# Down side of the second MoE: sum group in up-side banks, VectorE in GpSimd's place, and earlier splits

## The chip, the cores and the metric

One NeuronCore of a Trainium2 chip runs the whole program. The metric is the device time of one execution in microseconds; three executions of the kernel before were timed, and one more was profiled.

## The reference, cut to what matters

```python
x = attention(q, k, v, M_prev, z_prev, beta)      # 2304 tokens x 512
h = x @ w_in                                      # first MoE, 2048 wide
x = (h * sigmoid(h)) @ w_out
g = x @ w_gate                                    # second MoE, 1536 wide
val = x @ w_val
return ((g * sigmoid(g)) * val) @ w_out2          # 2304 x 512, float32
```

The change is in the last three lines, and in the pace at which the weights for them are prepared while the first MoE still runs.

## The kernel before, in words

The attention and the first MoE fill the first 680 us. While they run, the weights of the second MoE are read, combined and split into high and low halves, and written back to DRAM (`prep_w2`). A generator, `open_w2`, hands out that preparation over the last part of the first MoE: one step at every second call, set by `late=2` in the table `CFG`.

The second MoE works on three blocks of 768 tokens. Both of its sides are done with seven products of half-size matrices in place of eight (Strassen's scheme as Winograd has it), and each product is three matmuls: high by high, high by low and low by high half.

The up side has 12 slices `j` of 128 gate and 128 value columns. For each, `up(i, j, p)` issues the seven products, 6 matmuls of 384 columns each. Their sums live in PSUM: a tile of two banks (tag `o`, two tiles), and single banks `b` and `d` (two each, `sum_bank`). ScalarE copies a sum into a bank on which further products are added (L1205), VectorE adds others (L1213, L1219). A bank on which products are added to copied data needs a first matmul that marks it as written: the seed (L1182), for the first two slices of the first block. The gated results `r` are 128 x 384 tiles, two per slice (L1197).

The down side takes two slices together: for `q` from 0 to 5 the four tiles of slices 2q and 2q+1 are the quarters a11, a12, a21, a22. `halved` makes the three combinations of them on GpSimd (L1250 to L1252). `split_p` splits a tile into `ph` (a ScalarE cast, L1241) and `pl`, the low half (L1242, on GpSimd for the first product and for odd q, on VectorE for the others); S4 also takes a subtraction on VectorE (L1237). The products come in the order A11, S1, A12, S2, S4, S3, A22, six pieces each, 42 pieces a block. A piece is 9 matmuls of 256 columns (`piece_mm`, L1263): three token tiles by three halves. The products form four groups of sums, each in one tile `o` of two banks: A11 then A12, S1 then S4, S2 then S3, and A22. As there are two such tiles, the third group takes the one that the first leaves, and the first group ends with a ScalarE copy of the output (L1316).

The pieces of the first product are split in the up side; those of the others six pieces ahead, in rings of six `ph` and six `pl`. The last product of the last block is finished token tile by token tile, each followed by an addition (L1300) and a store.

TensorE's order is written out by `pe_order`: the products of neighbouring slices are interleaved, the first three pieces of a down side lie between the last products of the up side, and the last two between the first products of the next block. The order on the other engines and on SyncE's queue is made by a scheduler at build time. Weights come from DRAM by `stream` through a ring of eight 512 KB buffers, in the order of use (L1145); those of S2 and S4 are loaded once (`load_res`, L1155) and stay. `y_prep` loads and splits the inputs of the next block (L1022 to L1047) on ScalarE and VectorE.

Of the kernel before, what the change touches and what calls it, by code (L numbers as in the profile page):

```python
# [57 lines left out]
    late=2,  # L58
    res='S2 S4',
# [35 lines left out]
def kernel(  # L95
# [993 lines left out]
    def open_2():  # L1089
        ph2["xp"].close()  # L1090
        ph1.close()
        for nm in ("pr", "pp", "tp", "op", "res"):
# [3 lines left out]
    RES = CFG["res"].split()  # L1096
# [22 lines left out]
    def needs():  # L1119
        for n, (kind, i, x, y) in enumerate(pos):  # L1120
            if kind == "u":
                key = ("u", i, x, (0, 1, 1, 0, 2, 2, 3)[y])
            elif DQ[x] not in RES:
                key = ("d", i, x, y // 2)
            else:
                continue
# [21 lines left out]

    res = {}

    def load_res(g):
        for nm in RES:
            if g == 0:
                res[nm] = ph2["res"].tile([P, 2 * NJ2, 256], F32, name="res" + nm)
            nc.sync.dma_start(out=res[nm][:, 4 * g:4 * g + 4], in_=wdo[BW[nm], g])  # L1155
# [3 lines left out]
    def up(i, j, p):  # L1159
# [17 lines left out]
        def seeded(tag):  # L1177

            t = sum_bank(tag, "g" + tag)
            if i == 0 and j < 2:  # L1180
# [43 lines left out]
        else:  # L1224
# [3 lines left out]
            if j % 2:  # L1228
                halved(i, j // 2)

    pt, s1, queue, split = {}, {}, [], [0]

    def split_p(i, n, q):
        nm = DQ[n]
        a11, a12, a21, a22 = pt[0, 2 * q], pt[0, 2 * q + 1], pt[1, 2 * q], pt[1, 2 * q + 1]
        if nm == "S4":
            nc.vector.tensor_sub(a12, a12, a21)  # L1237
        src = dict(A11=a11, S1=s1.get(q), A12=a12, S2=a21, S4=a12, S3=a11, A22=a22)[nm]
        ph = ph2["pp"].tile([P, HT], F32R, tag="ph", name="ph", bufs=NJ2)
        pl = ph2["pp"].tile([P, HT], F32R, tag="pl", name="pl", bufs=NJ2)  # L1240
        nc.scalar.copy(ph, src)  # L1241
        (nc.gpsimd if n == 0 or q % 2 else nc.vector).tensor_sub(pl, src, f(ph))  # L1242
        return ph, pl

    def halved(i, q):

        queue.append(split_p(i, 0, q))
        a11, a21, a22 = pt[0, 2 * q], pt[1, 2 * q], pt[1, 2 * q + 1]
        s1[q] = ph2["pr"].tile([P, HT], F32, tag=f"s{q}", name="s1")
# [6 lines left out]
    def piece_mm(nm, g, q, pr, ts, begin, end):  # L1256
        ph, pl = pr
        w = res[nm][:, 2 * q:2 * q + 2] if nm in RES else streamed["d", g[0], DQ.index(nm), q // 2][:, 2 * (q % 2):2 * (q % 2) + 2]
        wh, wl = r_(w[:, 0]), r_(w[:, 1])
        for t in ts:  # L1260
            c = slice(P * t, P * t + P)
            for m, (a, x) in enumerate(((ph, wh), (ph, wl), (pl, wh))):
                nc.tensor.matmul(  # L1263
                    g[1][:, 256 * t:256 * t + 256], a[:, c], x, start=(begin and m == 0 and t != 1),
                    stop=(end and m == 2), skip_group_check=True,
                )

# [12 lines left out]
    def down(i, n, q):  # L1280
# [4 lines left out]
        if begin:  # L1285
            acc[G] = ph2["o"].tile([P, 1024], F32, tag="o", name=f"po{G}")[:, 0:3 * 256]
        g = acc[G]
        pr = queue.pop(0)
        if n == q == 0:
            split[0] = NJ2  # L1290
        if tail and q >= NJ2 // 2:
            late.append((q, pr))
# [3 lines left out]
            for t in range(HT // P):  # L1296
                for x, pr in late:
                    piece_mm(nm, (i, g), x, pr, (t,), False, x == q)
                c = slice(256 * t, 256 * t + 256)
                nc.vector.tensor_add(ot[:, c], g[:, c], snap["x"][:, c])  # L1300
                go(range(t, t + 1))
            return
        piece_mm(nm, (i, g), q, pr, range(HT // P), begin, q == NJ2 - 1)
        k = n * NJ2 + q
        while k > 2 and split[0] <= min(k + NJ2, len(DQ) * NJ2 - 1):
            queue.append(split_p(i, *divmod(split[0], NJ2)))
            split[0] += 1
# [4 lines left out]
        if nm in ("A11", "S1"):  # L1312
            nc.scalar.copy(s, g)
        elif nm == "A12":
            ot, go = put_out(i, 0, 0)
            nc.scalar.copy(ot, g)  # L1316
# [119 lines left out]
```

## Time and profile before

| | |
|---|---|
| median of 3 runs | 1096.02 us (1092.87 to 1096.34) |
| profiled execution | 1095.09 us, of which the span is 1092.9 |
| TensorE: matmul rows, weight loads | 1051.0 us (96%), 981.4 us (90%) |
| VectorE, ScalarE, GpSimd | 659.4, 554.8, 553.0 us |
| DMA | 252 MB, 231 GB/s on average |

The span is the time from the first to the last instruction. PE stands for TensorE's matmuls, PEld for its weight loads, which overlap them; DVE is VectorE, ACT ScalarE, POOL GpSimd, SP SyncE and SPq the queue of transfers that it issues. An engine's idle time before an instruction is put down to what it waited for last.

### The profile page before, as it was taken

The page shows a single profiled execution, that of the slowest core. Times are in us where ns is not written, and L with a number is a line of the kernel's source. Part 1 is how long each engine was busy: PE and PEld are TensorE (multiplying, and loading weights), DVE is VectorE, ACT ScalarE, POOL GpSimd, SP SyncE. Part 2 cuts the span into 40 slices and gives each one's busy share as a digit, 9 for nine tenths or more (in the row PEclk, how much of TensorE's full clock was granted, in tenths as well). Part 3 has the DMA queues.
Part 4 walks back from the last instruction along what each step waited for, and adds up shares of the span by engine and source line. Part 5 has one row for each costly group of instructions (what it writes and reads, how often), then busy time and mean ns, then how long its engine had stood idle before and what let it go on. Part 6 is the DMA issues. An engine that isn't in the chain of part 4 may idle for free.

```text
span 1092.9 us, 20747 instructions
## 1 busy us (share of the span) xinstructions
PE 1051.0 (96%) x7386; PEld 981.4 (90%) x7386; DVE 659.4 (60%) x1498; ACT 554.8 (51%) x1318; POOL 553.0 (51%) x622
## 2 busy tenths in 40 slices
PE   7889999999999998999999999999999999999998
PEld 5566888888999888998889999999999999999998
DVE  6897589996556656456757752344934449344443
ACT  6665677766655655546655542223532235322242
POOL 3676446577565565556644984122641226422253
PEclk8889999999999999999999999999999999999999
DMA  9967577565698554975537999877847778477771
GB/s 213 283 207 233 161 228 226 152 197 191 210 299 256 201 176 137 312 251 192 173 107 292 372 319 347 305 248 255 328 138 251 247 251 288 132 262 242 254 243 45
DMA packets 168103, 251.99 MB, mean 231 GB/s; under 512 B 76736, under 2 KB 114112, under 8 KB 168000
## 3 DMA queue, kind: packets, MB, share of 16 engines
q1 hardware_dynamic: 165824, 250.27, 69.3%
q8 instruction: 59, 0.97, 0.4%
q10 hardware_dynamic: 2176, 0.40, 0.2%
q14 instruction: 44, 0.36, 0.1%
HBM read 191.38 MB, written 59.24 MB: 229 GB/s over the span
## 4 chain that ended last, share of the span: by engine, by line
PE 68%; DVE 10%; DMA 7%; POOL 5%; issue 4%; ACT 2%; SPq 0%; POOLq 0%; ACTq 0%; DVEq 0%
PE h L825 12%; PE y L884 12%; PE po L1263 11%; PE oac L1171 10%; PE gb L1171 10%; PE gd L1171 3%; PE U L589 3%; PE pss L404 2%; PE pst L337 2%; DMA raw<-in_moe_w_val_dram 2%; POOL gl L835 1%; DMA raw<-in_moe_w_gate_dram 1%; DMA w<-wg 1%; POOL s L493 1%; DVE raw L702 1%
## 5 line engine op out<-in xcount | busy, mean ns | idle before, releaser
L825 PE MATMUL h<-xh,w 128*128 128x256 f32 (+1 forms) x1024 | 170.7, 305 | 7.3 <-ACT w L210 3.2
L884 PE MATMUL y<-gh,w 128*128 128x320 f32 (+1 forms) x1024 | 173.5, 305 | 3.6 <-DVE th L833 2.2
L1242 POOL TENSOR_TENSOR pl<-r,ph 128x384 fp32r<-128x384 f32 x63 | 69.1, 1100 | 199.4 <-ACT ph L1241 179.9
L835 POOL TENSOR_TENSOR gl<-th,gh 128x256 fp32r<-128x256 f32 (+1 forms) x128 | 111.4, 872 | 102.9 <-ACT gh L210 95.1
L825 PEld LDWEIGHTS h<-xh,w 128*128 128x128 f32 x1024 | 145.5, 191 | 15.2 <-ACT w L210 4.0
L884 PEld LDWEIGHTS y<-gh,w 128*128 128x128 f32 x1024 | 146.3, 190 | 10.1 <-DVE th L833 3.4
L1171 PE MATMUL gb<-yT,w 128*128 128x384 f32 x648 | 124.8, 336 | 0.0
L1171 PEld LDWEIGHTS gb<-yT,w 128*128 128x128 f32 x648 | 113.1, 188 | 0.0
L833 DVE SCALAR_TENSOR_TENSOR th<-th,h 128x256 f32<-128x256 f32 (+1 forms) x128 | 57.2, 449 | 74.8 <-ACT th L832 74.8
L1263 PE MATMUL po<-w,ph 128*128 128x256 f32 x540 | 98.2, 283 | 1.0 <-DVE ot L1300 1.0
L1241 ACT CAST ph<-r 128x384 fp32r<-128x384 f32 x108 | 55.0, 513 | 85.1 <-PE po L1263 45.7
L493 POOL TENSOR_TENSOR s<-s,r 128x128 f32<-128x128 f32 (+4 forms) x96 | 71.9, 775 | 49.7 <-DVE r L505 27.3
L884 PE MATMUL y<-gl,w 128*128 128x320 f32 (+1 forms) x512 | 94.0, 300 | 1.8 <-POOL gl L835 1.7
L825 PE MATMUL h<-xl,w 128*128 128x320 f32 (+1 forms) x512 | 92.8, 301 | 0.0
L460 ACT ACTIVATE s<-s,mn 128x128 f32<-128x128 f32 (+3 forms) x128 | 71.0, 556 | 31.9 <-DVE mn L456 31.4
L1263 PEld LDWEIGHTS po<-w,ph 128*128 128x128 f32 x540 | 84.9, 191 | 1.4 <-DVE ot L1300 1.4
L210 ACT CAST gh<-th 128x256 fp32r<-128x256 f32 (+1 forms) x128 | 55.1, 432 | 53.5 <-DVE th L833 41.6
L1171 PE MATMUL oac<-yB,w 128*128 128x384 f32 x432 | 81.3, 336 | 0.0
L884 PEld LDWEIGHTS y<-gl,w 128*128 128x128 f32 x512 | 76.6, 191 | 2.5 <-POOL gl L835 2.2
L1263 PE MATMUL po<-w,pl 128*128 128x256 f32 x270 | 76.4, 283 | 1.8 <-DVE pl L1242 1.8
L825 PEld LDWEIGHTS h<-xl,w 128*128 128x128 f32 x512 | 76.5, 191 | 1.7 <-issue 1.1
L1171 PEld LDWEIGHTS oac<-yB,w 128*128 128x128 f32 x432 | 75.4, 188 | 0.0
(165 smaller groups left out, 2228.5 us busy)
## 6 DMA issues: line engine op xcount, KB each, us to landing
w<-wg SPq DMA_DIRECT2D x108, 512.0 KB, 4.8
w<-wd SPq DMA_DIRECT2D x80, 512.0 KB, 5.4
wg<-wo SPq DMA_DIRECT2D x36, 512.0 KB, 3.4
wd<-w SPq DMA_DIRECT2D x32, 512.0 KB, 3.7
raw<-in_moe_w_out_dram SPq DMA_DIRECT2D x28, 512.0 KB, 4.9
w<-woT SPq DMA_DIRECT2D x27, 512.0 KB, 4.8
w<-wg SPq DMA_DIRECT2D x36, 256.0 KB, 4.9
w<-woB SPq DMA_DIRECT2D x18, 512.0 KB, 4.5
```

What stands on the lines that cost most here:

```text
L210: nc.scalar.copy(out, in_)
L460: nc.scalar.activation(out=a, in_=a, func=ACTF.Exp, scale=-1.0, bias=mn, accum_out=o["sm", sup][:, col:col + 1])
L493: nc.gpsimd.tensor_mul(a, a, r.to_broadcast([P, w]))
L589: run.append(lambda U=U, m=m, c=c, c0=c0, c1=c1, a=a, hh=hh, last=len(todo) - 1: nc.tensor.matmul(U[64 * hh:64 * hh + 64, c0:c1], row_of(" ...
L825: nc.tensor.matmul(ps[:, :nt], w[:, kk, :], x[:, kk, :nt], start=(m == 0), stop=(m == 3 * KD - 1))
L833: nc.vector.scalar_tensor_tensor(th[:, :nt], th[:, :nt], 1.0, ps[:, :nt], ALU.add, ALU.mult)
L835: tt(CFG["gl" if n >= CFG["n0"] else "gl0"]).tensor_sub(gl[:, :nt], th[:, :nt], f(gh[:, :nt]))
L884: nc.tensor.matmul(ps[:, :nt], w[:, c], g[:, :nt], start=(m == 0), stop=(m == last))
L1171: nc.tensor.matmul(dst, w[wi][:, P * kk:P * kk + P], y[ny][:, yi, kk], start=(start and m == 0), stop=(stop and m == 5), skip_group_check= ...
L1241: nc.scalar.copy(ph, src)
L1242: (nc.gpsimd if n == 0 or q % 2 else nc.vector).tensor_sub(pl, src, f(ph))
L1263: nc.tensor.matmul(g[1][:, 256 * t:256 * t + 256], a[:, c], x, start=(begin and m == 0 and t != 1), stop=(end and m == 2), skip_group_chec ...
```

## The change

- `late` goes from 2 to 3: a step of the weights' preparation at every third call.
- S2 and S4 are streamed like the others: `load_res` and its buffers are gone.
- `group` places the sums: the third group in two of the up side's `b` banks (two token tiles in one, the third in the other), the last product of the last block in three tiles (one `o` and two `d`), the others as before. `added` does an addition or copy for each such part.
- A `b` bank gets its seed in the first two slices of every block.
- Everything that GpSimd did here goes to VectorE.
- The rings hold 16. A11's pieces are split as soon as their tile is there, S1's as soon as it is summed, both in the up side; `refill` then splits as many further pieces as the ring has room for.

```diff
-    late=2,
-    res='S2 S4',
+    late=3,
+    ring=16,
...
-            if i == 0 and j < 2:
+            if j < 2 and (i == 0 or tag == "b"):
...
             if j % 2:
                 halved(i, j // 2)
+            else:
+                ring.append((0, j // 2))
+                queue[0, j // 2] = split_p(i, 0, j // 2)
...
     def split_p(i, n, q):
...
-        ph = ph2["pp"].tile([P, HT], F32R, tag="ph", name="ph", bufs=NJ2)
-        pl = ph2["pp"].tile([P, HT], F32R, tag="pl", name="pl", bufs=NJ2)
+        ph = ph2["pp"].tile([P, HT], F32R, tag="ph", name="ph", bufs=CFG["ring"])
+        pl = ph2["pp"].tile([P, HT], F32R, tag="pl", name="pl", bufs=CFG["ring"])
         nc.scalar.copy(ph, src)
-        (nc.gpsimd if n == 0 or q % 2 else nc.vector).tensor_sub(pl, src, f(ph))
+        nc.vector.tensor_sub(pl, src, f(ph))
...
     def halved(i, q):
-        queue.append(split_p(i, 0, q))
-        nc.gpsimd.tensor_sub(a11, a11, a21)
-        nc.gpsimd.tensor_add(s1[q], a21, a22)
-        nc.gpsimd.tensor_sub(a21, a22, a11)
+        nc.vector.tensor_add(s1[q], a21, a22)
+        ring.append((1, q))
+        queue[1, q] = split_p(i, 1, q)
+        nc.vector.tensor_sub(a11, a11, a21)
+        nc.vector.tensor_sub(a21, a22, a11)
+
+    def refill(i, k):
+        while len(ring) < len(DQ) * NJ2:
+            n = len(ring)
+            if n >= CFG["ring"]:
+                x, y = ring[n - CFG["ring"]]
+                if x * NJ2 + y > k:
+                    return
+            ring.append(divmod(n, NJ2))
+            queue[ring[-1]] = split_p(i, *ring[-1])
...
+    def group(kind):
+        if kind == "o":
+            t = ph2["o"].tile([P, 1024], F32, tag="o", name="po")
+            return [(t[:, 256 * x:256 * x + 256], x != 1) for x in range(3)], [(0, 3, t[:, 0:768])]
+        if kind == "b":
+            t0, t1 = sum_bank("b", "pb"), sum_bank("b", "pb")
+            return (
+                [(t0[:, 0:256], True), (t0[:, 256:512], False), (t1[:, 0:256], True)],
+                [(0, 2, t0[:, 0:512]), (2, 3, t1[:, 0:256])],
+            )
+        ts = [ph2["o"].tile([P, 1024], F32, tag="o", name="po")] + [sum_bank("d", "pd") for _ in range(2)]
+        return [(t[:, 0:256], True) for t in ts], [(x, x + 1, t[:, 0:256]) for x, t in enumerate(ts)]
...
-            acc[G] = ph2["o"].tile([P, 1024], F32, tag="o", name=f"po{G}")[:, 0:3 * 256]
+            acc[G] = group("b" if G == 2 else "t" if tail else "o")
...
-            nc.gpsimd.tensor_add(ot, s, snap["z"])
+            nc.vector.tensor_add(ot, s, snap["z"])
...
-                    if i == 0 and k % 6 == 0 and k < 18:
-                        load_res(k // 6)
```

On TensorE, where the third group of the first block starts (`po` are sums, `ph` and `pl` the halves of a piece), the order before was:

```order
L1263 MATMUL po0_10237<-w_10332,pl_10453 128x256
L1263 MATMUL po0_10237<-w_10332,ph_10452 128x256 x2
L1263 MATMUL po0_10237<-w_10332,pl_10453 128x256
L1263 MATMUL po2_10560<-resS2_10247,ph_10476 128x256 x2
L1263 MATMUL po2_10560<-resS2_10247,pl_10477 128x256
```

and it is now:

```order
L1267 MATMUL po_10258<-w_10353,pl_10395 128x256
L1267 MATMUL po_10258<-w_10353,ph_10394 128x256 x2
L1267 MATMUL po_10258<-w_10353,pl_10395 128x256
L1267 MATMUL pb_10595<-w_10355,ph_10398 128x256 x2
L1267 MATMUL pb_10595<-w_10355,pl_10399 128x256
```

No matmul has moved here, but the third group's are in a bank of the up side and take their weights from the stream.

On VectorE, at the change from the up to the down side of the first block (`y` tiles are prepared inputs, `s1` the sums of S1), the order before was:

```order
L1030 TENSOR_TENSOR yB22_10735<-ybot_10365,yB22_10735 128x768
L1242 TENSOR_TENSOR pl_10325<-s1_9860,ph_10324 128x384
L1197 SCALAR_TENSOR_TENSOR r_10278<-sg_10275,e_10191 128x384
L1197 SCALAR_TENSOR_TENSOR r_10297<-sg_10226,gb_10176 128x384
L1030 TENSOR_TENSOR yT4_10739<-yt_10366,yT4_10739 128x768
L1242 TENSOR_TENSOR pl_10346<-s1_10148,ph_10345 128x384
L1036 TENSOR_TENSOR yt_11846<-ytop_11844 128x768
L1242 TENSOR_TENSOR pl_10382<-r_9566,ph_10381 128x384
```

and it is now:

```order
L1030 TENSOR_TENSOR yB22_10760<-ybot_10378,yB22_10760 128x768
L1243 TENSOR_TENSOR r_10235<-r_10235,r_10219 128x384
L1186 SCALAR_TENSOR_TENSOR r_10295<-sg_10292,e_10208 128x384
L1186 SCALAR_TENSOR_TENSOR r_10314<-sg_10247,gb_10193 128x384
L1030 TENSOR_TENSOR yT4_10764<-yt_10379,yT4_10764 128x768
L1240 TENSOR_TENSOR s1_10316<-r_10219,r_10295 128x384
L1036 TENSOR_TENSOR yt_11872<-ytop_11870 128x768
L1244 TENSOR_TENSOR r_10219<-r_10295,r_10235 128x384
L1233 TENSOR_TENSOR pl_10319<-s1_10316,ph_10318 128x384
L1233 TENSOR_TENSOR pl_10334<-r_9567,ph_10333 128x384
```

The low halves of S1 that stood here are made earlier, but for the last; the combinations that GpSimd made have come in. Six more low halves, three subtractions and one 768-wide operation follow up to the first low half of S2.

On GpSimd, near the end of the first MoE (`gl` are low halves that TensorE needs, `S` and `wo` the preparation), the order before was:

```order
L835 TENSOR_TENSOR gl<-th,gh 128x256
L998 TENSOR_TENSOR S_8341<-t_8247 128x256
L1000 TENSOR_TENSOR S_8341<-t_8301,t_8247 128x256
L684 COPY raw_8442<-gl 128x1
L999 TENSOR_TENSOR S_8341<-t_8301,S_8341 128x256
L835 TENSOR_TENSOR gl<-th,gh 128x256
```

and it is now:

```order
L998 TENSOR_TENSOR S_8469<-t_8337 128x256
L1000 TENSOR_TENSOR S_8469<-t_8405,t_8337 128x256
L835 TENSOR_TENSOR gl<-th,gh 128x256
L952 TENSOR_TENSOR wo<-t_8337,wo 128x256
L999 TENSOR_TENSOR S_8469<-t_8405,S_8469 128x256
L835 TENSOR_TENSOR gl<-th,gh 128x256
```

The preparation's operations fall at other places between the low halves; their number is the same.

## Rows read from the trace of the kernel before

**Rows 1.** The page's busy times by engine, with share of the span and instructions.
```profile
PE 1051.0 (96%) x7386; PEld 981.4 (90%) x7386; DVE 659.4 (60%) x1498; ACT 554.8 (51%) x1318; POOL 553.0 (51%) x622
```

**Rows 2.** Windows by stage: bounds, length, busy us of each engine, clock, DMA.
```profile
core 0: us, PE busy (x) PEld busy (x) DVE busy (x) ACT busy (x) POOL busy (x), PEclk, DMA share, GB/s
600.00:680.00 80.00, 78.29 (x578) 77.53 (x577) 42.57 (x69) 33.55 (x75) 62.70 (x69) 1.00 0.95 343
767.00:815.00 48.00, 44.96 (x364) 44.56 (x363) 32.95 (x42) 24.60 (x46) 27.61 (x23) 1.00 0.63 228
815.00:901.00 86.00, 86.00 (x510) 86.00 (x509) 36.52 (x67) 25.37 (x53) 21.78 (x21) 1.00 0.75 253
901.00:949.00 48.00, 46.76 (x374) 46.56 (x374) 33.39 (x43) 25.56 (x48) 27.44 (x23) 1.00 0.62 206
1036.00:1093.00 57.00, 51.28 (x408) 50.46 (x406) 22.09 (x39) 21.76 (x42) 24.77 (x23) 1.00 0.43 148
```

**Rows 3.** Waits of the weight loads, 600 to 1093: us in total, times, longest.
```profile
PEld po L1263 <- ACT ot L1316: 4.3, 3, 1.4
PEld po L1263 <- DVE pl L1242: 2.0, 1, 2.0
PEld y L884 <- POOL gl L835: 1.9, 1, 1.9
PEld oac L1171 <- issue: 1.7, 1, 1.7
PEld po L1263 <- DVE ot L1300: 1.4, 2, 0.7
```

**Rows 4.** Waits of the matmul rows in the same stretch.
```profile
PE po L1263 <- ACT ot L1316: 3.7, 3, 1.2
PE po L1263 <- DVE pl L1242: 1.8, 1, 1.8
...
PE oac L1171 <- DMA w<-wg: 1.4, 1, 1.4
PE po L1263 <- DVE ot L1300: 1.0, 2, 0.5
```

**Rows 5.** The chain in order of time: start, us, what; a weight load, the pieces.
```profile
678.54 10.32 DMA w<-wg
...
793.28 24.02 PE po L1263 x198
```

**Rows 6.** Timeline of the up side, 12 weight loads: start, us, engine, line.
```profile
700.53 2.10 PEld L1171 LDWEIGHTS oac<-yB,w 128*128 128x128 f32 x12
```

**Rows 7.** Line 1155, the resident weights' six loads.
```profile
DMA to landing us min/median/max: 6.5/8.5/11.6
```

**Rows 8.** Windows with a full DMA, columns as in rows 2.
```profile
780.00:790.00 10.00, 8.20 (x69) 8.00 (x68) 9.97 (x9) 5.11 (x11) 8.02 (x7) 1.00 1.00 399
...
1035.00:1050.00 15.00, 15.00 (x111) 15.00 (x110) 7.78 (x14) 6.24 (x13) 7.33 (x7) 1.00 0.86 299
```

**Rows 9.** Groups by line, 1035 to 1093, VectorE's low halves.
```profile
L1242 DVE TENSOR_TENSOR pl<-r,ph 128x384 fp32r<-128x384 f32 x15 | 8.4, 563 | 19.3 <-ACT ph L1241 19.3
```

**Rows 10.** Groups by line, 766 to 812: busy us, mean ns of one, idle before.
```profile
L1242 DVE TENSOR_TENSOR pl<-r,ph 128x384 fp32r<-128x384 f32 x14 | 10.0, 728 | 11.5 <-ACT ph L1241 11.5
...
L1242 DVE TENSOR_TENSOR pl<-s,ph 128x384 fp32r<-128x384 f32 x3 | 3.3, 1096 | 0.0
...
L1242 POOL TENSOR_TENSOR pl<-r,ph 128x384 fp32r<-128x384 f32 x15 | 17.3, 1160 | 24.8 <-ACT ph L1241 24.8
```

**Rows 11.** Timeline around the first block's change of sides.
```profile
772.96 1.02 DVE L1030 TENSOR_TENSOR yB<-ybot,yB 128x768 fp32r<-128x768 f32 x1 [0.17 <-ACT yB L1029]
...
773.47 0.36 PEld L1263 LDWEIGHTS po<-w,ph 128*128 128x128 f32 x2
...
779.94 1.30 DVE L1036 TENSOR_TENSOR yt<-ytop 128x768 f32<-128x768 f32 x1 [0.39 <-DMA ytop<-yd]
```

**Rows 12.** Window in the first MoE's last part.
```profile
600.00:620.00 20.00, 18.29 (x136) 17.81 (x135) 14.53 (x19) 10.00 (x23) 19.94 (x23) 1.00 0.97 362
```

More of the change, by code (lines that the diff above doesn't have):

```diff
@@ L1229, in up @@
                 halved(i, j // 2)
-    pt, s1, queue, split = {}, {}, [], [0]
+            else:
+                ring.append((0, j // 2))
+                queue[0, j // 2] = split_p(i, 0, j // 2)
+    pt, s1, queue, ring = {}, {}, {}, []
     def split_p(i, n, q):
         nm = DQ[n]
-        a11, a12, a21, a22 = pt[0, 2 * q], pt[0, 2 * q + 1], pt[1, 2 * q], pt[1, 2 * q + 1]
         if nm == "S4":
-            nc.vector.tensor_sub(a12, a12, a21)
-        src = dict(A11=a11, S1=s1.get(q), A12=a12, S2=a21, S4=a12, S3=a11, A22=a22)[nm]
-        ph = ph2["pp"].tile([P, HT], F32R, tag="ph", name="ph", bufs=NJ2)
-        pl = ph2["pp"].tile([P, HT], F32R, tag="pl", name="pl", bufs=NJ2)
+            nc.vector.tensor_sub(pt[0, 2 * q + 1], pt[0, 2 * q + 1], pt[1, 2 * q])
+        src = s1[q] if nm == "S1" else pt[dict(A11=(0, 0), A12=(0, 1), S2=(1, 0), S4=(0, 1), S3=(0, 0), A22=(1, 1))[nm][0], 2 * q + (nm in ("A12", "S4", "A22"))]
+        ph = ph2["pp"].tile([P, HT], F32R, tag="ph", name="ph", bufs=CFG["ring"])
+        pl = ph2["pp"].tile([P, HT], F32R, tag="pl", name="pl", bufs=CFG["ring"])
@@ L1261, in piece_mm, with added @@
             c = slice(P * t, P * t + P)
+            dst, own_bank = g[t]
             for m, (a, x) in enumerate(((ph, wh), (ph, wl), (pl, wh))):
                 nc.tensor.matmul(
-                    g[1][:, 256 * t:256 * t + 256], a[:, c], x, start=(begin and m == 0 and t != 1),
-                    stop=(end and m == 2), skip_group_check=True,
-                )
+                    dst, a[:, c], x, start=(begin and m == 0 and own_bank), stop=(end and m == 2), skip_group_check=True,
+                )
+    def group(kind):
[10 more added lines that the diff above has]
+        return [(t[:, 0:256], True) for t in ts], [(x, x + 1, t[:, 0:256]) for x, t in enumerate(ts)]
+    def added(dst, parts, other=None):
+        for t0, t1, src in parts:
+            c = slice(256 * t0, 256 * t1)
+            if other is None:
+                nc.scalar.copy(dst[:, c], src)
+            else:
+                nc.vector.tensor_add(dst[:, c], src, other[:, c])
     def put_out(i, h, n):
@@ L1285, in down @@
         if begin:
-            acc[G] = ph2["o"].tile([P, 1024], F32, tag="o", name=f"po{G}")[:, 0:3 * 256]
[L1287 to L1290, printed above, removed]
+            acc[G] = group("b" if G == 2 else "t" if tail else "o")
+        g, parts = acc[G]
+        k = n * NJ2 + q
         if tail and q >= NJ2 // 2:
-            late.append((q, pr))
             if q < NJ2 - 1:
@@ L1296, in down @@
             for t in range(HT // P):
[L1297 to L1300, printed above, removed]
+                for x in range(NJ2 // 2, NJ2):
+                    piece_mm(i, n, x, g, queue[n, x], (t,), False, x == q)
+                added(ot, parts[t:t + 1], snap["x"])
                 go(range(t, t + 1))
             return
[L1303 to L1307, printed above, removed]
+        piece_mm(i, n, q, g, queue.pop((n, q)), range(HT // P), begin, q == NJ2 - 1)
+        if k > 2:
+            refill(i, k)
+        if k == len(DQ) * NJ2 - 1:
+            ring.clear()
         if q < NJ2 - 1:
@@ L1330, in down @@
             ot, go = put_out(i, 1, 0)
-            nc.vector.tensor_add(ot, g, snap["x"])
+            added(ot, parts, snap["x"])
             go()
-    late = []
     if True:
```

28 lines of the change are left out of this document (9 added, 19 removed).

## The prediction

> **What bounds the kernel now.** I read the busy times first [rows 1]. TensorE's matmul row is busy for 96% of the span and no other engine for more than 60%, so a microsecond is won only where TensorE stands still, or by giving it fewer matmuls. The windows by stage [rows 2] say where it stands: the clock share in the rightmost-but-two column is 1.00 throughout, the second block's up side (815 to 901) has weight loads for all of its 86 us, and each down side (767 to 815, 901 to 949, the last one within 1036 to 1093) has less than its length. So the second MoE is a full TensorE with a few holes in the down sides. Which holes these are is read from the list of waits of the weight loads after 600 us [rows 3]: 4.3 us in three waits for the ScalarE copy of A12's output, 2.0 us in one wait for a low half that VectorE made, 1.9 us in the first MoE for a low half of GpSimd's, 1.7 us in one wait put down to issue, 1.4 us in two waits for the last output's additions. The second MoE's share of these is 4.3 + 2.0 + 1.7 + 1.4 = 9.4 us.
>
> The matmul rows name the same waits shorter [rows 4]: 3.7, 1.8, 1.4 and 1.0, together 7.9 us. I take the weight loads, since a matmul's end is modelled and a load starts when the sequencer gets to it. The Trainium skill (Perfetto Trace Analysis, section Identifying the Most-Contended Engine) also holds matmul busy time for a bad measure, because matmuls are pipelined, and the busy share of LDWEIGHTS for the better one; by it the sum below stands, by the matmul rows it would be 1.5 us smaller.
>
> **The change part by part.**
>
> *Third group in two banks of the up side.* A12's sums and the third group's now lie in different tiles, so the first matmul of S2 no longer waits for the copy of A12's output, in any of the three blocks: -4.3 us [rows 3]. What would be late next there is S2's first low half (below) or its weights. The two banks are free: the up side's last product ends as the fourth piece starts, and S2 starts 15 pieces, 15 x 1.09 = 16 us, after that (a piece takes 1.09 us: 24.02 us for 198 matmuls, nine a piece [rows 5]). After S3 they must be read out before the next block's first seed; four pieces of A22 lie between, 4.4 us, and the additions start right away. Nothing there.
>
> *Seeds.* Two more matmuls in each of the second and third block, at 0.175 us (12 loads in 2.10 us [rows 6]): 4 x 0.175 = +0.7 us, on the path.
>
> *Tail.* The last product's three token tiles get a tile each, so the two waits for the additions of the tile before go: -1.4 us [rows 3]. The last addition and its store stay behind the last matmul as now.
>
> *No resident weights.* Six loads of 512 KB no longer stand on SyncE's queue ahead of the second block of up weights. Now these six land 6.5 to 11.6 us after issue [rows 7], and the load behind them takes 10.3 us [rows 5]; that is the wait of 1.7 us put down to issue, for the matmul row has it as a wait for this very load [rows 4]. Without them the load goes out some 5 us earlier into emptier queues: -1.7 us. In exchange S2 and S4 stream in every block: six loads a block. In the down side a load serves two pieces, 2.2 us, so the stream needs 0.524 MB / 2.2 us = 240 GB/s plus 1.2 MB of stores; the same rate runs now through A11, S1 and A12, together with the next block's inputs at 399 GB/s in the fullest stretch [rows 8], and the ring of eight puts a load out about 15 us ahead of use. Cost 0; bounds 0 and, should one load come late in each block by as much as that wait, +1.7 x 3 = +5.1. I take 0, since no load of the streamed products is waited for now.
>
> *GpSimd's work to VectorE, in the up side.* Per pair of slices VectorE gets two low halves and three combinations, 5 x 0.56 us [rows 9], 16.8 us a block. It is busy 36.5 of 86 us there [rows 2]; its operations on sums have several products of TensorE between themselves and the next reader, and the added ones come behind them in its order. ScalarE gets six casts more and is busy 25.4 of 86. Cost 0; the cover is that slack, and without it each pair would be late by at most its 2.8 us.
>
> *The same in the down side.* Now VectorE's low halves take 0.73 to 1.10 us on average in the first block, and GpSimd's 1.16 [rows 10]; in the last block, where the two engines take turns, VectorE's take 0.56 [rows 9]. The wait of 2.0 us comes from that crowd: late halves of A12. With the first two products split in the up side, 30 of 42 low halves are left, at 0.56 us against 1.09 us a piece on TensorE. The tight spot is the first block's start, where VectorE also prepares the inputs. By the changed order, counted from the low half at 772.96, which waits for TensorE's last use of its tile [rows 11], come two 768-wide operations at 1.02 and four narrow ones: 777.2. The next waits for its load until 779.94 [rows 11], and with it, one subtraction and the low half of S1's last piece it is 782.1. TensorE starts the fourth piece at 773.47 [rows 11], the twelfth 8 x 1.09 us later, and wants that low half 0.24 us on, at 782.4. So it is in time by 0.3 us. Ten narrow operations and one wide one later (788.7) S2's first low half is there, 1.3 us before its use at 790.0; after that VectorE gains on TensorE. So -2.0 us, and 0 for what is late next; bounds 0 and +2 in each of the first two blocks (again a wait as now). I take 0, for the count is made with full durations.
>
> *Preparation of the second MoE's weights taken every third step.* This reorders the end of the first MoE on GpSimd and TensorE. GpSimd is full there (19.94 of 20 us [rows 12]), and one late low half of it costs 1.9 us now [rows 3]. Two preparation operations still stand ahead of one GpSimd low half and two ahead of the next, so I take no change; bounds -1.9 (that wait goes) and +3.8 (two more like it).
>
> Sum: -4.3 - 1.4 - 1.7 - 2.0 + 0.7 = **-8.7 us**. The profiled execution took 1095.1 us (1092.9 of span and 2.2 around it), which gives 1086.4. It lies 0.9 us below the median of the runs shown, 1096.0, whose lowest and highest are 2.2 below and 1.2 above it. I predict 1086.5 us.
>
> **The rivals.**
>
> *A wait in place of the one removed.* At S2's start, or at S1's last piece, TensorE waits for VectorE in the first two blocks. For it: VectorE is busy 9.97 of 10 us in 780 to 790 [rows 8], and the margin above is 0.3 us. Against it: the additions come out in time at uncontended durations. At 2 us a block: 1086.5 + 4 = 1090.5. The Trainium skill (Perfetto Trace Analysis, section Optimizing Scalar/DVE Operations) speaks for giving a saturated VectorE's work to ScalarE or even to GpSimd, the reverse of this change, though it adds that the latter shares a read port with it and may not help; by its first half this rival is the outcome.
>
> *VectorE stays slow, and the change loses.* The long operations of the first two blocks also fall into the stretch where the DMA engines are full [rows 8]. If that, and not GpSimd, stretches them, they stay at 1.10 us [rows 10]. Then the 16 narrow ones up to S2 take 16 x 0.54 = 8.6 us longer, less 0.3 of margin, and S4's subtractions add 1.6: about 10 us a block, twice: 1086.5 + 20 = 1106. It decides from about 0.95 us an operation ((6 + 0.3) / 16 + 0.56), where it eats 12 us. Against it: in 1035 to 1050 the DMA share is 0.86 [rows 8], and the low halves of that block average 0.56 [rows 9]. The Trainium skill (SBUF — State Buffer, section Who interferes with whom) says that DMA never contends with a compute engine, and that a VectorE operation with two SBUF inputs does with a GpSimd one that reads SBUF; the rows of the last block bear it out.
>
> *The end of the first MoE gets worse.* Two more waits of 1.9 us: 1086.5 + 3.8 = 1090.3; for it the full GpSimd [rows 12], against it an unchanged amount of work there. The opposite, that wait gone, gives 1084.6.
>
> **How the numbers follow.** I give the forecast 0.66, the first rival 0.13, the second 0.06, the third 0.15. The range goes from 1082.5 (the forecast less 1.9 and the lower spread of the runs) to 1091.5 (the first or third rival, and 1 us of spread). It leaves out the slow VectorE, two rivals at once, and runs at the ends of the spread: about 2 in 10. A measurement of this kernel tells 0.3%, 3.3 us, from no change. Faster than 1092.7 are the forecast and most of the first and third rival: 0.86; within 0.3% fall the cases where these two come together (1086.5 + 4 + 3.8 = 1094.3): 0.08; slower is the second rival: 0.06.
>
> **What would show it.** Right: no wait of TensorE for the copy of A12's output or for the last additions, the third group's first matmul right behind A12's last, no wait above 0.3 us for a load at the start of the second MoE, VectorE's low halves at 0.56 us in all three down sides, GpSimd idle after the first MoE, four more seed matmuls. Wrong: waits for VectorE's low halves in the first two down sides, or the gain of the second MoE given back before 680 us.

## The result, and the profile after

The changed kernel takes 1085.63 us in the median (1084.32 to 1086.68, 6 runs) against 1096.18 us before (1092.87 to 1102.47, 6 runs): a ratio of 0.9900 with a 95% interval of 0.9869 to 0.9931. That is 10.5 us, where the interval allows 7.6 to 14.4. The prediction was 1086.5 us, 1082.5 to 1091.5.

The page's busy times after the change, which answer to [rows 1]:

```profile
PE 1046.1 (97%) x7390; PEld 977.5 (90%) x7390; DVE 702.7 (65%) x1633; ACT 547.0 (50%) x1318; POOL 405.7 (37%) x493
```

VectorE does 43 us more, GpSimd 147 us less: an operation on VectorE that runs undisturbed costs less than half of what it cost on GpSimd beside it (0.55 us below, 1.16 us in [rows 10]), and VectorE's own operations beside GpSimd have become shorter too. The weight loads have grown by four, the seeds.

The windows by stage, columns as in [rows 2]:

```profile
600.00:680.00 80.00, 78.91 (x586) 78.61 (x585) 40.38 (x71) 32.78 (x75) 60.59 (x70) 1.00 0.93 327
767.00:815.00 48.00, 48.00 (x390) 48.00 (x389) 31.20 (x59) 19.77 (x40) 0.00 (x0) 1.00 0.90 316
815.00:901.00 86.00, 86.00 (x504) 86.00 (x503) 53.44 (x100) 29.30 (x61) 0.00 (x0) 1.00 0.75 250
901.00:949.00 48.00, 48.00 (x391) 48.00 (x391) 29.20 (x55) 20.29 (x41) 0.00 (x0) 1.00 0.85 277
```

The second column of busy times is the weight loads: where they had 44.56 and 46.56 of 48 us in the two down sides, they now have all 48. GpSimd is idle, and the DMA share of the first down side has gone from 0.63 to 0.90, as S2 and S4 now stream through it.

The waits of the weight loads from 600 us to the end are these two, where [rows 3] shows the five largest kinds:

```profile
PEld y L884 <- DMA w<-wd: 1.3, 1, 1.3
PEld oac L1160 <- ACT gb L1194: 0.9, 1, 0.9
```

The second one is that of the very start of the second MoE; it stood in the kernel before too, with 0.9 us, and the change does not touch it. From there to the end the list has no wait of TensorE.

VectorE's low halves in the first down side (groups by line, 766 to 812), beside 0.73 to 1.10 us in [rows 10]:

```profile
L1233 DVE TENSOR_TENSOR pl<-r,ph 128x384 fp32r<-128x384 f32 x31 | 15.3, 549 | 0.0
```

In the second and the third down side (900 to 946, 1034 to 1083) they take as long:

```profile
L1233 DVE TENSOR_TENSOR pl<-r,ph 128x384 fp32r<-128x384 f32 x31 | 15.8, 556 | 2.4 <-ACT ph L1232 2.4
L1233 DVE TENSOR_TENSOR pl<-r,ph 128x384 fp32r<-128x384 f32 x30 | 15.8, 555 | 5.4 <-ACT ph L1232 5.4
```

**A ruler that is finer than the median.** The 10.5 us of the medians carry an uncertainty of 3 us and more, and most single parts of this change are smaller. Most of the scatter between the profiled executions lies at the front: in the first 200 us the granted clock of the profiled executions below is between 0.91 and 0.97 on average, and the same instruction of the first MoE, well before anything that the change moves on TensorE, starts anywhere from 565.0 to 571.7 us. So I measure from that instruction, a weight load of the first MoE that ends a wait of 0.34 or 0.35 us in every kernel, to the end of the span. The row in the timeline of the kernel before (start, us, engine, line, operation, idle time before it and what ended it):

```profile
567.58 0.66 PEld L825 LDWEIGHTS h<-xh,w 128*128 128x128 f32 x5 [0.35 <-ACT xh L210]
```

In the changed kernel:

```profile
568.55 0.54 PEld L825 LDWEIGHTS h<-xh,w 128*128 128x128 f32 x4 [0.35 <-ACT xh L210]
```

And in a second profile of the changed kernel:

```profile
567.03 0.66 PEld L825 LDWEIGHTS h<-xh,w 128*128 128x128 f32 x5 [0.35 <-ACT xh L210]
```

With spans of 1092.9, 1083.4 and 1082.2 us the stretch is 525.3, 514.9 and 515.2 us long. The change is worth 10.2 to 10.5 us on it, and two profiles of one kernel differ by 0.3. Each row below is one profiled execution for the stretch, and six or twelve runs for the median. The ratios compare with runs of the kernel before that were timed beside each row, whose medians were 1096.18 us (the first two rows), 1093.42 (changed again; the same, slice ahead), 1095.39 (all streamed, `late=2`, no early splits, `late=4`) and 1094.76 (the others). So two medians of this table are not to be subtracted from each other where these differ. The repeat of the changed kernel gained 9.2 us against its 1093.42.

| kernel | starts at, us | stretch, us | median, us | ratio to before, 95% |
|---|---|---|---|---|
| before | 567.58 | 525.3 | 1096.18 | |
| changed | 568.55 | 514.9 | 1085.63 | 0.9869 to 0.9931 |
| changed, again | 567.03 | 515.2 | 1084.20 | 0.9890 to 0.9932 |
| before, no GpSimd | 565.34 | 521.8 | 1092.09 | 0.9956 to 0.9985 |
| before, third group moved | 570.53 | 521.1 | 1090.39 | 0.9956 to 0.9987 |
| before, all streamed | 565.73 | 524.5 | 1094.46 | 0.9978 to 1.0010 |
| changed, sums back | 565.63 | 520.3 | 1091.79 | 0.9959 to 0.9995 |
| changed, some low halves on GpSimd | 565.62 | 515.9 | 1085.38 | 0.9907 to 0.9937 |
| changed, `late=2` | 565.01 | 516.2 | 1084.39 | 0.9881 to 0.9920 |
| changed, no early splits | 565.90 | 514.8 | 1083.23 | 0.9869 to 0.9912 |
| the same, slice ahead | 567.93 | 513.9 | 1083.75 | 0.9877 to 0.9930 |
| changed, slice ahead, `late=4` | 571.72 | 529.5 | 1093.63 | 0.9958 to 1.0006 |

### The profile page after: what moved, and what is told of

It reads as the page before. It is cut to its first block, busy times and chain, and to the rows that moved or that the text cites. A ratio compares the mean times of both kernels' runs of the same rounds, so it can differ in the third digit from the quotient of the medians.

```text
span 1083.4 us, 20669 instructions
## 1 busy us (share of the span) xinstructions
PE 1046.1 (97%) x7390; PEld 977.5 (90%) x7390; DVE 702.7 (65%) x1633; ACT 547.0 (50%) x1318; POOL 405.7 (37%) x493
## 4 chain that ended last, share of the span: by engine, by line
PE 70%; DVE 9%; POOL 6%; DMA 5%; issue 4%; ACT 2%; SPq 0%; POOLq 0%; DVEq 0%; ACTq 0%
PE h L825 12%; PE y L884 11%; PE oac L1160 10%; PE gb L1160 10%; PE po L1267 9%; PE pb L1267 4%; PE gd L1160 3%; PE pss L404 3%; PE U L589 2%; PE pst L337 2%; POOL gl L835 2%; DMA raw<-in_moe_w_gate_dram 2%; DMA raw<-in_moe_w_val_dram 1%; POOL s L493 1%; DVE t L702 1%
## 5 line engine op out<-in xcount | busy, mean ns | idle before, releaser
L825 PE MATMUL h<-xh,w 128*128 128x320 f32 (+1 forms) x1024 | 169.8, 303 | 7.6 <-DVE yp L889 2.7
L1267 PE MATMUL po<-w,ph 128*128 128x256 f32 x516 | 93.8, 283 | 0.0
L1267 PEld LDWEIGHTS po<-w,ph 128*128 128x128 f32 x516 | 81.2, 191 | 0.0
L1232 ACT CAST ph<-r 128x384 fp32r<-128x384 f32 x108 | 51.1, 512 | 55.9 <-DVE r L1186 35.6
L1267 PE MATMUL po<-w,pl 128*128 128x256 f32 x258 | 73.0, 283 | 0.0
L832 ACT ACTIVATE th<-h 128x256 f32<-128x256 f32 (+1 forms) x128 | 51.3, 404 | 33.5 <-PE h L825 20.0
```

What stands on the lines that cost most here:

```text
L825: nc.tensor.matmul(ps[:, :nt], w[:, kk, :], x[:, kk, :nt], start=(m == 0), stop=(m == 3 * KD - 1))
L832: nc.scalar.activation(out=th[:, :nt], in_=ps[:, :nt], func=ACTF.Tanh, scale=0.5 / WS)
L1267: nc.tensor.matmul(dst, a[:, c], x, start=(begin and m == 0 and own_bank), stop=(end and m == 2), skip_group_check=True,)
```

## The experiments

The theory is the prediction's: the change removes four kinds of waits of TensorE, each with a cause of its own, and their sum is the gain. Against it stand its rivals (VectorE becomes the bound, the full DMA and not GpSimd stretches VectorE's operations) and the doubt whether the parts add up, or whether one of them does it all.

### One part at a time, on the kernel before

**GpSimd's work to VectorE, nothing else** (rings of six, old times of splitting):

```diff
-        (nc.gpsimd if n == 0 or q % 2 else nc.vector).tensor_sub(pl, src, f(ph))
+        nc.vector.tensor_sub(pl, src, f(ph))
...
-        nc.gpsimd.tensor_sub(a11, a11, a21)
-        nc.gpsimd.tensor_add(s1[q], a21, a22)
-        nc.gpsimd.tensor_sub(a21, a22, a11)
+        nc.vector.tensor_sub(a11, a11, a21)
+        nc.vector.tensor_add(s1[q], a21, a22)
+        nc.vector.tensor_sub(a21, a22, a11)
...
-            nc.gpsimd.tensor_add(ot, s, snap["z"])
+            nc.vector.tensor_add(ot, s, snap["z"])
```

> The kernel before with GpSimd's work of the second MoE on VectorE, in the old ring of six and with the old times of splitting. If the crowd alone made the wait of 2.0 us for a low half of A12 in the first block, it goes: 1094.0 us, the low halves of all three blocks at 0.56 us. If splitting earlier is what removed it, VectorE is behind at the start of the first down side as before, since it gets 18 more low halves and three combinations for each pair: a wait of 1 to 4 us stays in the first block, and may show in the second: 1095 to 1100 us. All other waits stay (three of 1.4 us for the copy of A12's output, 1.7 us at the start of the second MoE, two of 0.7 us at the end).

Measured: 3.6 us less on the stretch. The waits of its weight loads from 600 us on:

```profile
PEld po L1263 <- ACT ot L1316: 4.2, 3, 1.4
PEld y L884 <- POOL gl L835: 1.9, 1, 1.9
PEld po L1263 <- DVE ot L1300: 1.4, 2, 0.7
PEld oac L1171 <- ACT gb L1205: 0.9, 1, 0.9
PEld y L884 <- ACT gh L210: 0.4, 2, 0.3
PEld oac L1171 <- issue: 0.3, 1, 0.3
```

The wait for a low half is gone without any earlier split, and VectorE's low halves take 0.55 to 0.56 us on average in all three down sides: the crowd alone made it. That is 2.0 us of the 3.6. Most of the rest is the wait put down to issue, 0.3 us in place of 1.7, which I had not expected to move; the six resident loads land 5.4 to 8.8 us after issue here, 6.5 to 11.6 in [rows 7]. The kernel with only the third group moved has 1.2 us at that place. So this wait scatters between executions, and a single profile sizes it badly.

**The third group in two banks, and its seeds, nothing else:**

```diff
-            if i == 0 and j < 2:
+            if j < 2 and (i == 0 or tag == "b"):
...
-            acc[G] = ph2["o"].tile([P, 1024], F32, tag="o", name=f"po{G}")[:, 0:3 * 256]
+            if G == 2:
+                t0, t1 = sum_bank("b", "pb"), sum_bank("b", "pb")
+                acc[G] = [t0[:, 0:256], t0[:, 256:512], t1[:, 0:256]], [(0, 512, t0[:, 0:512]), (512, 768, t1[:, 0:256])]
+            else:
...
```

> The kernel before with only the third group's sums moved to two banks of the up side, and the four seed matmuls. If the parts add up, 4.3 - 0.7 = 3.6 us less than before: 1092.5 us, the three waits of 1.4 us gone, the wait of 2.0 us for a low half at its place. The rival, that another wait takes their place (VectorE is late with S2's first low half, in the first two blocks, as long as the crowd is there), expects waits of 0.5 to 1.4 us for a low half at S2's start in two blocks: 1093.5 to 1095.5 us.

Measured: 4.2 us less on the stretch. The three waits for ScalarE are gone, and the waits for low halves of the first block are now three:

```profile
PEld po L1263 <- DVE pl L1242: 1.3, 2, 0.9
...
PEld pb L1263 <- DVE pl L1242: 0.5, 1, 0.5
```

Together they are 1.8 us, about the 2.0 that stood there; the last, 0.5 us, is inside the third group, so a part of the rival is true as long as GpSimd is in VectorE's way. With 4.3 off, 0.7 on for the seeds, 0.2 off for the low halves and 0.5 off for the wait put down to issue, which scatters, the sum is 4.3 off, against 4.2 measured. So about 3.5 of the 4.2 us are this part's own.

**S2 and S4 streamed, nothing else:**

```diff
-    res='S2 S4',
+    res='',
...
```

> The kernel before with S2 and S4 streamed, and no other part of the change. If the six resident loads ahead on SyncE's queue make TensorE wait at the start of the second MoE, the load behind them lands 3 us or more before its use, the wait of 1.7 us there goes to under 0.3 us, and nothing else changes: 1.7 us less than before. The rival, that the queues are full then anyway from the end of the first MoE, expects 1 to 1.7 us of waiting for the same load, and no change. If streaming costs something, waits for loads appear in the down sides.

Measured: the wait of 1.7 us is gone altogether, and the stretch is only 0.9 us shorter. TensorE reaches the late low half of the first down side 1.6 us earlier (108.6 us behind the second MoE's first weight load, 110.2 before), and its wait there is the same 2.0 us, so nothing of the gain is lost to VectorE. What follows that wait differs. Windows of this kernel, just before the wait and behind it:

```profile
782.00:784.00 2.00, 2.00 (x19) 2.00 (x19) 2.00 (x2) 0.99 (x2) 1.32 (x2) 1.00 1.03 385
...
786.20:789.00 2.80, 2.80 (x14) 2.80 (x15) 2.76 (x6) 0.51 (x1) 0.00 (x0) 0.54 0.29 114
```

The kernel before, in the wait of the same length and behind it:

```profile
787.60:790.00 2.40, 0.60 (x6) 0.40 (x5) 2.40 (x4) 0.51 (x1) 1.01 (x1) 1.00 0.90 340
790.00:792.00 2.00, 2.00 (x16) 1.84 (x16) 2.00 (x5) 0.51 (x1) 0.00 (x0) 1.00 0.35 141
```

The granted clock, third from the right, is 0.54 behind the wait in the one execution, which is nearly the lower of its two levels (1.2 of 2.4 GHz), and 1.00 in the other. From the load behind the wait to the first load of S2 it is 4.75 us here (786.20 to 790.95) and 3.40 in the kernel before (789.88 to 793.28): the wait cost 1.35 us more than its own length. Streaming costs no wait for a load, as forecast, and this lower clock is what hides most of its gain on the stretch. Why it came in this execution and not in the other is open; in the medians this kernel cannot be told from the one before.

### One part at a time, undone in the changed kernel

**The third group's sums back in a tile of the down side, without the added seeds:**

```diff
-            if j < 2 and (i == 0 or tag == "b"):
+            if i == 0 and j < 2:
...
-            acc[G] = group("b" if G == 2 else "t" if tail else "o")
+            acc[G] = group("t" if tail else "o")
```

> The changed kernel with the third group's sums back in a two-bank tile of the down side, and without the four added seed matmuls; all else as changed. If the tile is what made TensorE wait, three weight-load waits of about 1.4 us for the ScalarE copy of A12's output come back at S2's start, 4.3 us, less 4 x 0.175 = 0.7 us of seeds: about 1089.2 us against 1085.6, and 0.993 of the kernel before. The rival, that the waits were part of the crowd on VectorE and ScalarE, now gone, expects waits under 0.5 us there and 1085 to 1086 us.

Measured: 5.4 us more on the stretch, which is more than the 3.6 expected (and a ratio of 0.998 to the kernel before, not 0.993), because the first of the three waits is longer:

```profile
PEld po L1267 <- ACT ot L1289: 6.2, 3, 3.3
```

ScalarE's timeline around that wait:

```profile
784.29 0.52 ACT L1232 CAST ph<-r 128x384 fp32r<-128x384 f32 x1 [0.92 <-DVE r L1228]
785.23 2.17 ACT L1232 CAST ph<-r 128x384 fp32r<-128x384 f32 x5 [0.42 <-DVE r L1228]
787.30 0.79 ACT L1289 COPY ot<-po 128x768 f32<-128x768 f32 x1
```

The copy that frees the tile stands behind casts of pieces far ahead, some of which wait for S4's subtractions on VectorE. In the second and the third block the wait is 1.44 us, as in the kernel before, and with rings of six and no GpSimd (the first run above) it is 1.4 us at most in all three. Splitting up to 16 pieces ahead puts work in front of the copy, which costs 1.9 us in the first block, and the separate banks make that harmless: 6.2 - 0.7 = 5.5 us. The rival is out: all three waits are back although GpSimd is idle.

**The low halves of odd pieces of the last five products on GpSimd again:**

```diff
-        nc.vector.tensor_sub(pl, src, f(ph))
+        (nc.gpsimd if n > 1 and q % 2 else nc.vector).tensor_sub(pl, src, f(ph))
```

> The changed kernel with the 15 low halves of odd pieces of A12, S2, S4, S3 and A22 of each block on GpSimd again; combinations and early splits stay as changed. If GpSimd is what stretches VectorE's operations, the VectorE low halves of the first down side go from 0.55 us on average to 0.65 us or more, and those on GpSimd take about 1.1 to 1.2 us; with splits up to 16 pieces ahead TensorE waits for none of them, or at most 1 us in all: 1085.6 to 1086.6 us. If the full DMA stretches them, VectorE's stay at 0.55 us, for DMA's share of that down side is 0.90 in the changed kernel too. The view that GpSimd itself made the wait of 2.0 us expects a wait of 1 to 2 us in the first block: 1087 to 1088 us.

The groups by line of the first down side (766 to 812):

```profile
L1233 POOL TENSOR_TENSOR pl<-r,ph 128x384 fp32r<-128x384 f32 x15 | 19.3, 1314 | 107.3 <-DMA w<-woB 102.3 <-ACT ph L1232 3.1 <-PE pb L1267 2.0
L1233 DVE TENSOR_TENSOR pl<-r,ph 128x384 fp32r<-128x384 f32 x16 | 14.5, 956 | 0.0
```

Its window, columns as in [rows 2]:

```profile
767.00:815.00 48.00, 47.54 (x381) 46.80 (x380) 32.86 (x40) 18.24 (x39) 19.28 (x15) 1.00 0.83 295
```

VectorE's low halves go from 0.549 to 0.956 us as soon as GpSimd works beside it, and GpSimd's take 1.31. Half of the work has left VectorE, and its 16 operations take 14.5 us where all 31 took 15.3. The DMA share is 0.83 here and 0.90 in the changed kernel, so the DMA is less full where VectorE is slower, and the full DMA is not the cause. TensorE waits for low halves three times, 1.0 us in all, and the stretch is 1.0 us longer (0.7 against the repeat of the changed kernel); the medians cannot show that. The waits:

```profile
PEld po L1267 <- DVE pl L1233: 0.6, 2, 0.4
...
PEld pb L1267 <- DVE pl L1233: 0.4, 1, 0.4
```

**The preparation at every second call again:**

```diff
-    late=3,
+    late=2,
```

> The changed kernel with a step of the weights' preparation at every second call, as before; all else as changed. If the pace is what shortened the end of the first MoE, the wait of 1.9 us for a low half of GpSimd comes back at 611 us and the wait of 1.3 us for a load of the first MoE's weights goes: about 1.1 us from 567 us to the second MoE's first matmul more than in the changed kernel, 1086.7 us. If the pace does nothing and the difference is scatter, the stretch has the length that it has in the changed kernel, within 0.3 us.

Measured: 1.0 to 1.3 us more on the stretch, and the wait that the kernel before had is back:

```profile
PEld y L884 <- POOL gl L835: 1.9, 1, 1.9
```

From the ruler's start to the second MoE's first weight load it is 112.1 us before, 112.2 here, 110.9 and 111.3 in the two profiles of the changed kernel: the pace is worth 0.8 to 1.2 us. The wait for GpSimd goes, and one for a load of the first MoE's weights (1.3 and 1.6 us) takes part of its place.

**No early splits:** rings of six, all pieces but A11's split six ahead, and everything else as changed (the kernel before with the edits above, `late=3`, and a tile for each token tile of the last product).

> The changed kernel without its early splits: rings of six, A11's pieces split when both slices are done, all others six pieces ahead; third group in two banks, last product in three tiles, all streamed, no GpSimd in the second MoE, the new pace. If GpSimd's absence alone frees VectorE, as in the kernel before without it, this is as fast as the changed kernel: 1085.6 us, waits for low halves under 1 us in all. If the early splits carry a part of the gain, waits for low halves of 0.5 to 2 us stand at S1's end or S2's start of the first two blocks: 1086.6 to 1089.6 us.

Measured: 514.8 us, the same as the changed kernel. Its waits from 600 us on:

```profile
PEld y L884 <- DMA w<-wd: 1.0, 1, 1.0
PEld oac L1171 <- ACT gb L1205: 0.9, 1, 0.9
PEld y L884 <- POOL gl L835: 0.2, 1, 0.2
```

No wait for a low half anywhere. The ring of 16 and the splits in the up side carry nothing of the change's gain that a stretch can show.

### Trying to go further

**The first block's second slice begins earlier, and the preparation comes at every fourth call:**

```diff
-    late=3,
+    late=4,
...
-        return [x for _, x in sorted(got)]
+        got = [(1.5 if x == ("u", 0, 1, 0) else z, x) for z, x in got]
+        return [x for _, x in sorted(got)]
```

> The changed kernel with two edits that lie apart in the trace. First, the first product of the first block's second slice is taken two products earlier, ahead of the product that waits for ScalarE's copy at the start of the second MoE: the wait of 0.9 us there goes, if its weights are there in time; if not, a wait for a load of 0.5 to 2 us takes its place. Second, a step of the weights' preparation at every fourth call in place of every third: if GpSimd's preparation is what makes TensorE wait at the end of the first MoE, the waits there (1.3 us for a load) stay or shrink; if the preparation now comes too late, TensorE waits for the second MoE's first weights, several us. Together 1084 to 1086 us if right, up to 1092 if the preparation is late.

Measured: 529.5 us on the stretch, 15 us worse than the changed kernel. This profiled execution, with 1102.96 us, is the slowest of twelve; their median, 1093.63, is 9 to 10 us above the kernels with `late=2` and without early splits that were timed on the same chip, and 1.6 above the range that I gave. Every fourth call is too late: in this execution GpSimd and ScalarE still prepare weights up to 690 us, and TensorE waits in four places for ScalarE's high halves and then once for 4.4 us, for a copy that ScalarE itself holds back for 5.3 us until the last prepared weights are written:

```profile
PEld y L884 <- ACT gh L210: 5.1, 4, 2.7
PEld oac L1161 <- ACT e L1199: 4.4, 1, 4.4
```

Two windows behind the two longest of these waits:

```profile
685.00:690.00 5.00, 5.00 (x23) 5.00 (x22) 0.00 (x0) 1.52 (x3) 5.00 (x7) 0.58 0.37 136
...
700.00:705.00 5.00, 4.88 (x15) 4.88 (x16) 1.68 (x3) 0.56 (x2) 0.00 (x0) 0.50 1.03 392
```

Behind each the granted clock is at or near its lower level for 5 us: by an estimate from these shares (5 x 0.42 and 5 x 0.50) about 2.1 and 2.5 us are lost against the full clock, so such a wait is in good part paid a second time. The slice ahead has no share in it, for the next run has it, on the kernel without early splits, and none of these waits.

**The slice ahead alone, on the kernel without early splits** (the second of the two edits above, at `late=3`):

> The kernel of the run without early splits (rings of six), and in the first block the first product of the second slice taken ahead of the first slice's second product, at the old-new pace of every third call. The wait of 0.9 us for ScalarE's copy at the start of the second MoE goes, if that slice's first weights are there by then: 514.4 us from the load behind the 0.35 us wait at 565 to 568 us to the end of the span, against 515.3 to 515.4 in the changed kernel and in the run without early splits; 1083 to 1085 us. If the weights are late, a wait for a load of 0.5 to 2 us stands in its place and the stretch is 515 to 517 us.

(The lengths in this expectation and the next count from the load in front of the wait, 0.5 us before the row of the table: 514.4 there is 513.9 here.) Measured: 513.9 us, as expected, 0.9 us less than without it. The wait is gone; the start of the second MoE in the timeline of its weight loads:

```profile
678.80 1.03 PEld L1172 LDWEIGHTS oac<-yB,w 128*128 128x128 f32 x6
679.82 0.19 PEld L1183 LDWEIGHTS gb<-yB,w 128*128 128x128 f32 x1
679.99 1.05 PEld L1172 LDWEIGHTS oac<-yB,w 128*128 128x128 f32 x6
```

The second slice's first six loads follow at once, where the changed kernel stands for 0.92 us. In the median, 1083.75 against 1084.20 us for the changed kernel on the same chip, this cannot be told apart; on the stretch it is the shortest of all.

**The changed kernel again, beside it,** without an edit:

> The changed kernel itself, on the same chip as the run with the slice ahead. The stretch from the load behind the 0.35 us wait at 565 to 568 us to the end of the span is 515.4 us again, within 0.5 us, while that load itself starts up to 3 us earlier or later, since the first 200 us run at a granted clock that differs from execution to execution; the median is 1084 to 1087 us.

Measured: 515.2 us, 0.3 more than the first profile, with a start 1.5 us earlier.

## Why the prediction was right

It forecast a gain of 8.7 us against its profiled execution; the stretch shows 10.5, and 10.2 in the repeat. The forecast put all of it into the second MoE. From that one's first weight load (at 679.67 us before, at 679.48 and 678.34 in the two profiles of the changed kernel) to the end of the span it is 413.2 us before and 403.9 in both profiles after, so 9.3 us; the rest lies in the first MoE. That the median, 1085.63, came out within 0.9 us of the 1086.5 says less than it seems, for the interval of the gain is 7 us wide. Term by term:

| term | forecast | shown |
|---|---|---|
| third group in two banks | -4.3 | three waits gone; about -4.5 by the rows below |
| seeds | +0.7 | four more loads; +0.35 a block by the rows below |
| tail | -1.4 | two waits gone in every kernel with the new tail, there in every one with the old |
| resident loads | -1.7 | wait gone in all nine profiles without them; 0.3, 1.2 and 1.7 us in three with them |
| VectorE's crowd | -2.0 | wait gone without GpSimd, also without early splits |
| end of the first MoE | 0 | -0.8 to -1.2, from the pace |

The first two terms can be read without the scatter, from S2's first weight loads in the first and the second block. Before:

```profile
793.28 0.30 PEld L1263 LDWEIGHTS po<-resS,ph 128*128 128x128 f32 x2 [1.44 <-ACT ot L1316]
...
927.56 0.30 PEld L1263 LDWEIGHTS po<-resS,ph 128*128 128x128 f32 x2 [1.44 <-ACT ot L1316]
```

In the changed kernel:

```profile
787.91 0.31 PEld L1267 LDWEIGHTS pb<-w,ph 128*128 128x128 f32 x2
...
921.03 0.31 PEld L1267 LDWEIGHTS pb<-w,ph 128*128 128x128 f32 x2
```

From one to the next it is 134.28 us before and 133.12 after, and again 134.28 with the sums back and the seeds gone. So a block gains 1.16 us, which is one wait of 1.51 from start to start (below) less two seeds at 0.175.

The term of the resident loads is right in its cause, and its size is that of one execution: with the resident loads the wait also came out at 0.3 and 1.2 us, so it is partly luck how well the -1.7 carries over to the median.

The one term that was clearly off is the last: the prediction took no change from it, with bounds of -1.9 and +3.8, because the two rows of GpSimd's order that it compared looked alike. The late low half did go, but a wait for a weight load came in its place, so neither the zero nor the -1.9 was right.

A second miss is small and runs through all terms: I took a wait's price as the idle time in the list of waits. In the kernel before, at the first of the tail's two waits, the timeline reads:

```profile
1085.46 0.19 PEld L1263 LDWEIGHTS po<-w,pl 128*128 128x128 f32 x1
...
1086.37 0.30 PEld L1263 LDWEIGHTS po<-w,ph 128*128 128x128 f32 x2 [0.72 <-DVE ot L1300]
```

From start to start it is 0.91 us, where loads otherwise follow each other every 0.12: the wait cost 0.79 us, not 0.72, since the idle time begins only when the load before has ended. At 0.07 us more each (1.44 so becomes 1.51), six such waits in the down sides add 0.4 us. With this the second MoE's 8.7 come to 9.1 of the 9.3 measured, and with the first MoE's 0.8 to 1.2 the whole to 9.9 to 10.3 us of the 10.2 to 10.5.

The tight spot was judged rightly, and a little too strictly. VectorE's rows in the first block:

```profile
778.21 0.96 DVE L1036 TENSOR_TENSOR yt<-ytop 128x768 f32<-128x768 f32 x1 [3.36 <-DMA ytop<-yd]
779.08 0.55 DVE L1244 TENSOR_TENSOR r<-r 128x384 f32<-128x384 f32 x1
779.55 0.55 DVE L1233 TENSOR_TENSOR pl<-s,ph 128x384 fp32r<-128x384 f32 x1
...
785.11 1.02 DVE L1233 TENSOR_TENSOR pl<-r,ph 128x384 fp32r<-128x384 f32 x2
```

The low halves' first use in the timeline of the weight loads:

```profile
780.59 0.19 PEld L1267 LDWEIGHTS po<-w,pl 128*128 128x128 f32 x1
...
788.15 0.19 PEld L1267 LDWEIGHTS pb<-w,pl 128*128 128x128 f32 x1
```

VectorE waits for the load as foreseen, and makes the low half of S1's last piece at 780.10, 0.5 us before TensorE wants it (forecast 0.3); S2's first is done at 785.66, 2.5 us ahead (forecast 1.3). The difference is that operations in a row start every 0.47 us, not every 0.56. The count began at a low half that was to wait for TensorE; its row has it waiting for a ScalarE cast [rows 11], which changes nothing in the sum, as the row's own time was taken.

**The rivals.** A wait in place of the one removed did not come in the changed kernel; it came, at 0.5 us, where the third group was moved alone and GpSimd stayed. That the full DMA keeps VectorE slow has fallen: 0.549 us at a DMA share of 0.90, where [rows 10] had 0.73 to 1.10, and 0.956 with GpSimd back. The Trainium skill (SBUF — State Buffer, section Who interferes with whom) says both, that DMA stays out of it and that a two-input VectorE operation collides with a GpSimd one that reads SBUF; the runs agree. The Trainium skill's advice to offload a saturated VectorE even to GpSimd (Perfetto Trace Analysis, section Optimizing Scalar/DVE Operations) comes with the doubt that it might not help. Here the doubt was the right half of that advice: VectorE has no free time in the 10 us from 780 of the changed kernel, and half of its low halves on GpSimd made TensorE wait 1.0 us more. The window, columns as in [rows 2]:

```profile
780.00:790.00 10.00, 10.00 (x86) 10.00 (x85) 10.00 (x22) 5.66 (x13) 0.00 (x0) 1.00 0.97 360
```

The end of the first MoE got better, not worse.

One reason in the prediction was beside the point: it counted the splits in the up side among the causes that bring the low halves in time. The kernel without them is as fast on the stretch, and has no such wait.

## What to carry to other kernels

Before moving work off a busy VectorE to GpSimd, look at the duration of the same operation where GpSimd is idle: here half of the work on GpSimd made the other half take three quarters longer. A wait taken away need not show its own length: the 1.7 us of the resident loads were worth 0.9 alone, since in that execution the clock fell behind the wait that came next. A deeper look-ahead can make a wait longer, as it did where the tile that TensorE needed was shared. When single parts are smaller than the scatter of the total, measure from an instruction that all kernels share behind the noisy part; two profiles then agreed to 0.3 us, where the two medians of that kernel differed by 1.4.

## What the runs showed that was not expected

- The granted clock behind a wait of 2.0 us was 0.54 for 2.8 us in one execution and 1.00 in another, at the same place of the program; behind waits of 2.7 and 4.4 us it was 0.58 and 0.50 over 5 us. The wait of 2.0 us with the lower clock behind it cost two thirds as much again as it shows.
- VectorE's 128 x 384 operations last 0.55 us each but start every 0.47 us when they stand in a row, so full durations overstate a queue of them by a sixth.
- The mean granted clock of the first 200 us was 0.91 to 0.97, and the place of the same instruction at 565 to 572 us went with it: 570.5 and 571.7 at 0.91 and 0.93, 565.0 to 568.6 at 0.94 to 0.97.
- How long the loads behind the six resident ones take to land scattered enough to make a wait of 0.3, 1.2 or 1.7 us at one place, and nothing in the kernels there explains it; what else used the queues was not tried.
